# Attention beside a long convolution: the filters asked for among the first loads, and zero products on score banks

## The chip, the cores and the metric

The kernel runs on one core of a Trainium2 chip. The metric is device time of one execution in microseconds (us). "TensorE", "VectorE", "ScalarE", "GpSimd" and "SyncE" are the engines; the profile calls them PE (PEld for its weight loads), DVE, ACT, POOL and SP. A "q" behind the name, as in SPq, is the engine's queue issuing a transfer.

## The reference

Two independent halves, their outputs side by side. Length S = 2048, width D = 512, all in bf16.

```python
def _A_ref(x, wqkv, wo):                       # attention, H = 32 heads of 16
    q, k, v = (x @ wqkv), cut in three and into heads
    p = softmax(q k^T * 16 ** -0.5)
    return (p v) as (S, D) @ wo

def _B_ref(q, k, v, shift_k, ssm_k, ssm_D):    # gated long convolution, per channel
    k_shift[s] = sum over t < 4 of k[s - 3 + t] * shift_k[:, t'] 
    kv = k_shift * v
    y = causal convolution of kv with ssm_k (2048 taps per channel), + kv * ssm_D
    return q * y

out = concatenate([A, B], axis=-1)
```

## The kernel before

**Attention.** The scores are 2048 blocks of 128 keys by 512 queries, in 32 groups (4 query blocks by 8 groups of 4 heads). They are taken in *chunks* T of 3 blocks (2 in every second chunk up to `N_EARLY` = 56), 695 in all. For each chunk `emit_qk` issues the score products (L719) into PSUM banks 0 to 2 or 3 to 5 in turn, and ScalarE takes the exponential of the chunk into a tile PT (L726). From T = 16 on VectorE takes over one block of some chunks, by arithmetic of its own (L744 first, then the six passes of L784 to L791), in sets of two, later four; `dve_choice` decides by how far VectorE is behind in the plan. `emit_pv` (L835) multiplies the results with V into bank 6 (bank 7 for one group).

**Projections.** Jobs of Q, K and V products (`pe_unit` L401 and L408, `v_mm` L452) run in bank 5 early on, in bank 7 later, between score products; VectorE evicts them (L444, L462, L430). A job's next product waits until the bank is evicted.

**Convolution filters.** The filters `ssm_k` (512 channels by 2048 taps, 2 MB) come in two halves, `KZN[0]` (in tile QT) and `KZN[1]` (in tile EI), 1 MB each, with `DSS` (the 512 values of `ssm_D`, tile JNK). All three add to one semaphore, d_kz, and `h_kzl` is the third one's full count. GpSimd puts the first 128 taps into a small tile KZ0 and adds `DSS` (`kz_first`, L502 and L503). VectorE then turns the filters in 16 pieces of two halves each (`kz_turn`, L512 and L518) into a tile in WR, from where SyncE stores them to a scratch tensor in DRAM. The convolution (L992) reads shifted views of that scratch from T = 128 on.

**Order.** The program is written by a planner in plain Python. Every engine has a clock in it (`pe.t`, `act.t`, `dve.t`); each operation is appended to its engine's queue with a planned duration, and `when_of(h)` is the planned time of a result. On the chip each queue runs in order, waiting on semaphores. A transfer's planned landing is 4.0 us after its issue unless given. The pieces of the filters are appended at the end of a chunk's round:

```python
        while kv_pieces and T >= kv_pieces[0][0]:
            kv_pieces.pop(0)[1]()
        while kz_pieces and T >= kz_pieces[0][0] and (dve.t + kz_pieces[0][1] <= end + KZ_OVER or T >= kz_pieces[0][0] + 4):
            kz_pieces.pop(0)[2]()
```

`kv_pieces` holds `kz_first`, for T = 8. The `kz_pieces` are due at T = `KZ_AT` + 3i + j for piece i, half j, with `KZ_AT` = 11.

**First loads.** SyncE asks for: x rows 0 to 511, the transposes of x 512 to 1023, the second parts of WQ and WK (columns from 128), the transposes of x 1024 to 1535, `KZN[0]`, `KZN[1]`, `DSS`, the last transposes of x, then transposes of k and rows of v. ScalarE asks for: the first parts of WQ and WK, WV, the shift taps SHK; its table load and its first work stand behind these in its queue.

**Padding.** `keep_share` (L1160) adds products of zeros into a bank that is being accumulated, when the plan has TensorE busy under `SHARE` = 0.9 of the last `SPAN` = 3.4 us. `filler_home` names the bank, or None: between two groups, where the old group's last and the new group's first products with V are not both under way, there often is none, and nothing is added.

Of the kernel before, what the change touches and what calls it, by code (L numbers as in the profile page):

```python
# [6 lines left out]
ALU = mybir.AluOpType  # L7
# [35 lines left out]
N_EARLY = 56  # L43
# [38 lines left out]
SPAN = 3.4  # L82
SHARE = 0.9
# [14 lines left out]
SET_US = 0.72  # L98
PART_US = 0.6
KZ_US = .57  # L100
KZ_AT = 11
KZ_OVER = 0.0
FINISH = 8
TURN_BLKS = 9
TURN_AFTER = 4
STALL = 0.3
# [90 lines left out]
def bass_concat_heads__mha_block__ssm_conv_h3__prompt_kernel(  # L197
# [21 lines left out]
    def sem(name):  # L219
        return enter(nc.semaphore(name))  # L220
# [18 lines left out]
    ZR = sb("ZR", [128, 32])  # L239
# [4 lines left out]
    IDN = sb("IDN", [128, 128])  # L244
# [4 lines left out]
    KZ0 = sb("KZ0", [128, 4, 192])  # L249
# [31 lines left out]
    def dma(eng, dsem, outp, inp, deps=(), transpose=False, us=4.0, takes=0.0):  # L281
        h = dsem.add()

        def fn(e):
            f = e.dma_start_transpose if transpose else e.dma_start
            f(outp, inp).then_inc(dsem.sem, 16)  # L286
# [10 lines left out]
    def when_of(h):  # L297
        return at[(id(h[0]), h[1])] if h else 0.0
# [5 lines left out]
    d_tap, d_kz, d_wo = [DmaSem(sem(n)) for n in ("d_tap", "d_kz", "d_wo")]  # L304
# [18 lines left out]
    def load_x(sc):  # L323
        for c in range(4):
            h = turn_in(d_x[sc], xT[:, c, sc * 512:(sc + 1) * 512], x2[sc * 512:(sc + 1) * 512, 128 * c:128 * c + 128])
        h_x[sc] = [h]

    load_x(1)
    h_wv = dma(act, d_w[2], WV, wview[:, :, 2 * D:3 * D])
    h_shk = dma(act, d_tap, SHK[:, :, :], B_shift_k.rearrange("(c p) m -> p c m", p=128))  # L330
    h_wq.append(dma(sp, d_w[3], WQ[:, :, 128:D], wview[:, :, 128:D]))
    h_wk.append(dma(sp, d_w[4], WK[:, :, 128:D], wview[:, :, D + 128:2 * D]))
    load_x(2)
    kzview = B_ssm_k.rearrange("(p c) s -> p c s", c=4)
    for i in range(2):
        dma(sp, d_kz, KZN[i], kzview[:, 2 * i:2 * i + 2, :])
    h_kzl = dma(sp, d_kz, DSS, B_ssm_D.rearrange("(p c m) -> p c m", c=4, m=1))
    load_x(3)
    h_kt = {0: turn_in(d_kt[0], KTR[0][:, 16:LKT], k2[:, 0:128])}
    h_v2 = {0: dma(sp, d_v[0], VLO, v2[0:1024, :].rearrange("(t p) d -> p t d", p=128))}  # L340
# [154 lines left out]

    h_kzw = [None]

    h_kzt, h_kzs = [None], {}

    def kz_first():  # L500
        for i in range(2):
            h = pool.op(lambda e, i=i: e.tensor_copy(KZ0[:, 2 * i:2 * i + 2, 64:192], KZN[i][:, :, 0:128]), [h_kzl])  # L502
        h_kzt[0] = pool.op(lambda e: e.tensor_tensor(KZ0[:, :, 64:65], KZ0[:, :, 64:65], DSS, ALU.add), [h])  # L503

    def kz_turn(i, half):
        c, ro = i // VG, i % VG
        g0, g1 = (0, 24) if half == 0 else (24, NGR)
        o = 255 - ro - VG * g0
        k = KZN[c // 2][:, c % 2, o:o + 1]
        k = bass.AP(tensor=k.tensor, offset=k.offset, ap=[k.ap[0], [-VG, g1 - g0], [128, NB - 1], [-1, VG]])  # L510
        hs = [h_kzl, h_kzs.get(i - 4)]
        h = dve.op(lambda e: e.tensor_copy(KZS[:, i % 4, g0:g1, 1:NB, :], k), hs, us=KZ_US)  # L512
# [5 lines left out]
        h_kzp[i] = dve.op(lambda e: e.tensor_copy(KZS[:, i % 4, :, 0, :], k0), [h_kzt[0], h_kz0] + hs, us=0.19)  # L518
        kz_store(i)
        if i == 7:  # L520
            load_vhi()
# [17 lines left out]
    kz_pieces = [(KZ_AT + 3 * i + j, KZ_US + 0.22 * j, lambda i=i, j=j: kz_turn(i, j)) for i in range(16) for j in range(2)]  # L539
    kv_pieces.sort(key=lambda x: x[0])  # L540


# [19 lines left out]
    h = k_part(0, 128)  # L562
# [132 lines left out]
            chunk_of[b] = (T, j)  # L695
        chunks.append((bl, banks_of[T]))

    h_exp = {}
    h_blk = {}
    h_ptfree, pt_used = {}, {}  # L700

# [8 lines left out]
    def emit_qk(T):  # L710
        bl, banks = chunks[T]
        deps = qk_deps(T)
        assert None not in deps or T < 8

        def fn(e):
            ins = None
            for b, bank in zip(bl, banks):
                qb, g, kt, s = blk(b)
                ins = e.matmul(PS[:, bank, :],  # L719
                               lhsT=KTo[32 * s:32 * s + 32, g // 2, kt * 128:(kt + 1) * 128],  # L720
                               rhs=QT[32 * s:32 * s + 32, qb % 2, g, :],
                               start=True, stop=True, tile_position=(32 * s, 0))
            return ins
        h = pe.op(fn, deps, us=0.32)
        n = len(bl) - (bl[-1] in on_dve)
        h_exp[T] = act.op(lambda e: e.activation(PT[:, T % R_PT, 0:n * QB],  # L726
                                                 PS[:, banks[0]:banks[0] + n, :].rearrange("p b f -> p (b f)"),
                                                 ACT.Exp, scale=math.log(2.0) / OCT),
                          [h] + h_ptfree.get(T - R_PT, []), us=0.41 * n + 0.1)
# [415 lines left out]

    def keep_share(T, lim):
        home = filler_home(T)
        if home is None or T >= NT:
            return
        bank, col, start, dep = home  # L1150
        busy = sum(u for t, u in pe.last if t > lim - SPAN)
        n = blk_group(rest[0]) if rest else NQB * NG - 1
        turning = len(rest_of[n]) < 9 or len(rest_of[n]) > 4 * KT - 9
        us = min(lim - pe.t - 0.13, (1.0 if turning else SHARE) * SPAN - busy)
        while us > 0.08:
            k = min(max(int((us - 0.02) / 0.0565), 1), (512 - col) // 128)
# [6 lines left out]
            pe.op(fn, [h_zr, h_idn, dep], us=0.02 + 0.0565 * k)  # L1163

    def emit_bg(T, lim):
        bg_step(T, lim)
# [146 lines left out]
    for T in range(NT + 3):  # L1313
        if T < NT:
            take(T)
            for b in chunks[T][0]:
                pv_todo[blk_group(b)].append(b)
            emit_qk(T)
        lim = max(when_of(d) for d in qk_deps(T + 1)) if T + 1 < NT else pe.t + 1.0
        pvs = due_pvs(T, lim)  # L1320
        for b in [b for batch in pvs for b in batch]:
            n = blk_group(b)
            pv_todo[n].remove(b)
            pv_left[n] -= 1
            if not pv_left[n]:
                pv_done[n] = T
        early = False
        for batch in pvs:
            n = blk_group(batch[0])
            ready = max([when_of(h_blk[b]) for b in batch]  # L1330
                        + [when_of(bank_free[pvb(n)]) for b in batch if not in_bank.get((n, blk(b)[3]))])
            if T >= N_EARLY and not early and ready > pe.t + STALL:
                early = True
                emit_bg(T, ready)
            emit_pv(batch, T)
        if early:
# [90 lines left out]
```

## Time and profile before

| | |
|---|---|
| median of 3 runs | 832.82 us (829.57 to 833.69) |
| the profiled execution | 830.77 us |
| its span, first to last instruction | 828.9 us |
| ScalarE busy | 810.6 us (98%) |
| VectorE busy | 787.6 us (95%) |
| TensorE busy | 719.2 us (87%) |
| mean granted TensorE clock | 0.994 of full |

In the profile's rows a bracket such as [2.84 <-DMA JNK] is how long the engine stood idle ahead of the row, and what ended that. In rows of the timeline the first number is the start, the second the length that the merged instructions cover, both in us. In rows by line the numbers behind the bar are busy us, mean ns of one instruction, and idle us ahead of them. In rows by stretch (A:B) the busy times of PE, PEld, DVE, ACT and POOL stand in this order, then the granted clock, the share of the DMA engines, and GB/s.

### The profile page before, as it was taken

Reading aid. Unit: us, or ns where it says so; the run is one execution under the profiler, and the core shown is the slowest. Engines: PE = TensorE matmul, PEld = TensorE weight load, DVE = VectorE, ACT = ScalarE, POOL = GpSimd, SP = SyncE. Lnnn points to the kernel's source line nnn. Section 1 sums busy time; section 2 is a strip of 40 time slices with the busy share of each in tenths; the row PEclk is TensorE's granted clock in tenths of the full one; section 3 lists DMA queues with packets and bytes.
Section 4 is the critical chain, followed back from the end, with each engine's and each line's share of the span. In section 5 each row is a group of like instructions: output and inputs, shape, how many; then the busy total and the mean of one; then the engine's idle time right before and its main releaser. Section 6 shows DMA issues by size and latency. Waiting matters only on the chain.

```text
span 828.9 us, 29863 instructions
## 1 busy us (share of the span) xinstructions
PE 719.2 (87%) x13409; PEld 320.7 (39%) x13445; DVE 787.6 (95%) x1228; ACT 810.6 (98%) x702; POOL 17.3 (2%) x35
## 2 busy tenths in 40 slices
PE   8788899988888888888888888888888888988997
PEld 3233333334433443344344444344444443444222
DVE  3799999999999999999999999999999999999995
ACT  7899999999999999999999999999999999999997
POOL 3000000000000000000000000000000000000000
PEclk9999999999999999999999999999999998999999
DMA  9977602048736756499768788787789988775100
GB/s 244 288 253 269 178 1 48 30 98 282 235 95 195 219 184 216 138 259 296 233 210 274 234 260 263 231 254 238 226 264 307 274 286 299 229 225 187 26 1 26
DMA packets 123855, 167.30 MB, mean 202 GB/s; under 512 B 50384, under 2 KB 55504, under 8 KB 123472
## 3 DMA queue, kind: packets, MB, share of 16 engines
q1 hardware_dynamic: 120752, 162.77, 63.5%
q8 instruction: 106, 1.74, 0.8%
q10 hardware_dynamic: 2400, 1.05, 0.5%
q0 software_dynamic: 576, 1.57, 0.5%
q14 instruction: 21, 0.17, 0.1%
HBM read 143.14 MB, written 16.52 MB: 193 GB/s over the span
## 4 chain that ended last, share of the span: by engine, by line
ACT 88%; DVE 6%; PE 3%; SPq 2%; DMA 1%; issue 0%; POOL 0%; DVEq 0%
ACT PT L726 88%; DVE WR L512 2%; SPq L286 2%; DMA JNK<-in_B_ssm_D_dram 1%; PE PS L719 1%; PE PS L835 1%; DVE EI L744 1%; DVE KTo L444 0%; DVE KV L487 0%; DVE EA L787 0%; DVE WR L518 0%; DVE VAF L462 0%; PE PS L916 0%; DVE EA L784 0%; DVE EI L791 0%
## 5 line engine op out<-in xcount | busy, mean ns | idle before, releaser
L726 ACT ACTIVATE PT<-PS 128x1536 bf16<-128x1536 f32 (+1 forms) x695 | 806.5, 1432 | 7.3 <-PE PS L719 6.8
L719 PE MATMUL PS<-QT,KTo 32*128 32x512 bf16 x2048 | 273.0, 386 | 91.0 <-ACT PT L726 67.6
L835 PE MATMUL PS<-PT,VAF 128*32 128x512 bf16 x1782 | 227.8, 391 | 1.0 <-DVE STG L883 0.4
L992 PE MATMUL PS<-WR,KV 128*8 128x64 bf16 (+15 forms) x8192 | 182.7, 213 | 0.2
L992 PEld LDWEIGHTS PS<-WR,KV 128*18 128x18 bf16 (+15 forms) x8192 | 150.1, 119 | 43.9 <-issue 22.5
L719 PEld LDWEIGHTS PS<-QT,KTo 32*128 32x128 bf16 x2048 | 69.3, 91 | 243.2 <-ACT PT L726 224.0
L744 DVE TENSOR_SCALAR EI<-PS 128x512 int32<-128x512 f32 x206 | 136.6, 684 | 1.9 <-PE PS L719 1.2
L791 DVE SCALAR_TENSOR_TENSOR EI<-EI,EA 128x1024 int32<-128x1024 int32 (+1 forms) x90 | 92.1, 1040 | 0.0
L835 PEld LDWEIGHTS PS<-PT,VAF 128*32 128x32 bf16 x1782 | 53.4, 93 | 90.0 <-issue 84.0
L1160 PE MATMUL PS<-ZR,IDN 128*128 128x512 bf16 (+3 forms) x290 | 79.6, 329 | 0.2 <-issue 0.2
L790 DVE TENSOR_TENSOR EA<-EA,xT 128x1024 bf16<-128x1024 f16 (+1 forms) x53 | 46.7, 895 | 0.0
L835 PE MATMUL PS<-EI,VAF 128*32 128x512 bf16 x206 | 45.1, 411 | 1.8 <-DVE VAF L462 1.2
L787 DVE TENSOR_TENSOR EA<-EA,xT 128x1024 f16<-128x1024 f16 (+1 forms) x53 | 46.6, 896 | 0.0
L744 DVE TENSOR_SCALAR xT<-PS 128x512 int32<-128x512 f32 x60 | 39.9, 686 | 0.5 <-PE PS L719 0.2
L784 DVE TENSOR_SCALAR xT<-EI 128x1024 f16<-128x1024 uint16 (+1 forms) x46 | 37.8, 849 | 0.4
L1160 PEld LDWEIGHTS PS<-ZR,IDN 128*128 128x128 bf16 x290 | 22.7, 97 | 30.5 <-issue 20.4
L791 DVE SCALAR_TENSOR_TENSOR EI<-EI,WKV 128x1024 int32<-128x1024 int32 x28 | 34.1, 1219 | 0.0
L788 DVE TENSOR_SCALAR xT<-xT 128x1024 f16<-128x1024 f16 (+1 forms) x53 | 27.0, 527 | 0.0
L786 DVE TENSOR_SCALAR EA<-xT 128x1024 f16<-128x1024 f16 (+1 forms) x53 | 26.7, 527 | 0.0
L790 DVE TENSOR_TENSOR WKV<-WKV,STG 128x2048 bf16<-128x2048 f16 x21 | 25.5, 1215 | 0.0
L787 DVE TENSOR_TENSOR WKV<-WKV,STG 128x2048 f16<-128x2048 f16 x21 | 25.5, 1212 | 0.0
L883 DVE STREAM_TRANSPOSE STG<-PS 128x512 f32<-128x512 f32 x31 | 22.0, 711 | 2.8 <-PE PS L835 2.6
(87 smaller groups left out, 498.9 us busy)
## 6 DMA issues: line engine op xcount, KB each, us to landing
WR<-kz_scratch SPq DMA_DIRECT2D x512, 256.0 KB, 4.1
kz_scratch<-WR SPq DMA_DIRECT2D x16, 752.0 KB, 4.2
QN<-in_B_q_dram SPq DMA_DIRECT2D x16, 128.0 KB, 4.5
out_dram<-KV SPq DMA_DIRECT2D x16, 128.0 KB, 4.7
out_dram<-OUTA POOLq DMA_DIRECT2D x12, 128.0 KB, 3.7
QT<-in_B_ssm_k_dram SPq DMA_DIRECT2D x1, 1024.0 KB, 5.6
EI<-in_B_ssm_k_dram SPq DMA_DIRECT2D x1, 1024.0 KB, 8.8
STG<-in_B_v_dram SPq DMA_DIRECT2D x1, 1024.0 KB, 7.3
```

The lines of the kernel that those rows point to most:

```text
L719: ins = e.matmul(PS[:, bank, :], lhsT=KTo[32 * s:32 * s + 32, g // 2, kt * 128:(kt + 1) * 128], rhs=QT[32 * s:32 * s + 32, qb % 2, g, :], ...
L726: h_exp[T] = act.op(lambda e: e.activation(PT[:, T % R_PT, 0:n * QB], PS[:, banks[0]:banks[0] + n, :].rearrange("p b f -> p (b f)"), ACT.E ...
L744: s.fix.append(dve.op(lambda e: e.tensor_scalar(ei_of(i)[:, 0, :], PS[:, bank, :], FIX_LO, FIX_ADD, ALU.max, ALU.add), [h] + old + [x for ...
L784: step(2, lambda sl: lambda e: e.tensor_scalar(eb[:, sl], frac[:, sl], FS / OCT, -FS * ROOT0, ALU.mult, ALU.add), s.fix + old)
L786: step(4, lambda sl: lambda e: e.tensor_scalar(ea[:, sl], eb[:, sl], FS * (ROOT0 - ROOT1), None, ALU.add))
L787: step(2, lambda sl: lambda e: e.tensor_tensor(ea[:, sl], ea[:, sl], eb[:, sl], ALU.mult))
L788: step(4, lambda sl: lambda e: e.tensor_scalar(eb[:, sl], eb[:, sl], C1 * BITS / FS ** 3, (C0 + C1 * ROOT0) * BITS / FS ** 2, ALU.mult, AL ...
L790: step(2, lambda sl: lambda e: e.tensor_tensor(eg[:, sl], ea[:, sl], eb[:, sl], ALU.mult))
L791: step(1, lambda sl: lambda e: e.scalar_tensor_tensor(ei[:, sl], ei[:, sl], BITS / OCT, eg[:, sl], ALU.mult, ALU.add), ends=True)
L835: ins = e.matmul(PS[32 * s:32 * s + 32, pvb(qb * NG + g), :], lhsT=VAF[:, kt, h * VW:h * VW + 32], rhs=rhs, start=(order[b] == 0), stop=(o ...
L992: ins = e.matmul(PS[32 * c:32 * c + NW - 2 * n, BGB, col:col + 64], lhsT=KV[:, 2 * n:NW, 4 * qd + c], rhs=w, start=(n == 0), stop=(n == NB ...
L1160: return e.matmul(PS[:, bank, col:col + 128 * k], lhsT=IDN[:, :], rhs=ZR[:, :].rearrange("p (m d) -> p m d", m=1).broadcast_to([128, 4 * k ...
```

## The change

The two filter halves get a semaphore each. `DSS` and `KZN[0]` are asked for by ScalarE, behind SHK; `KZN[1]` by SyncE, behind the first transposes of x. The second x transposes come next, and the second parts of WQ and WK behind them. The planned landings of the halves are given, 11.5 and 14.5 on the plan's clock. `kz_first` is cut in two, one for each half, at T = 2 and T = 4. The pieces start at T = 4 in place of 11, in the same steps of three chunks, and each waits for its own half; a piece is appended only once the plan's VectorE clock has reached the half's planned landing less 0.1.

The second part: where `filler_home` gives None and T is 56 or more, zero products are added onto the first bank of the chunk's scores, behind the score products and ahead of the exponential, which then waits for them too. One is added as long as it ends in the plan 0.14 us before the exponential starts, and the busy share is under 0.9.

```diff
-KZ_AT = 11
+KZ_AT = 4
+KZ_LANDS = 11.5, 14.5
+ZERO_GAP = .14
...
     load_x(1)
     h_wv = dma(act, d_w[2], WV, wview[:, :, 2 * D:3 * D])
     h_shk = dma(act, d_tap, SHK[:, :, :], B_shift_k.rearrange("(c p) m -> p c m", p=128))
+    kzview = B_ssm_k.rearrange("(p c) s -> p c s", c=4)
+    dma(act, d_kz[0], DSS, B_ssm_D.rearrange("(p c m) -> p c m", c=4, m=1))
+    h_kzl = []
+    for i, q in enumerate((act, sp)):
+        h_kzl.append(dma(q, d_kz[i], KZN[i], kzview[:, 2 * i:2 * i + 2, :], us=KZ_LANDS[i] - q.t))
+    load_x(2)
     h_wq.append(dma(sp, d_w[3], WQ[:, :, 128:D], wview[:, :, 128:D]))
     h_wk.append(dma(sp, d_w[4], WK[:, :, 128:D], wview[:, :, D + 128:2 * D]))
-    load_x(2)
-    kzview = B_ssm_k.rearrange("(p c) s -> p c s", c=4)
-    for i in range(2):
-        dma(sp, d_kz, KZN[i], kzview[:, 2 * i:2 * i + 2, :])
-    h_kzl = dma(sp, d_kz, DSS, B_ssm_D.rearrange("(p c m) -> p c m", c=4, m=1))
     load_x(3)
...
-    def kz_first():
-        for i in range(2):
-            h = pool.op(lambda e, i=i: e.tensor_copy(KZ0[:, 2 * i:2 * i + 2, 64:192], KZN[i][:, :, 0:128]), [h_kzl])
-        h_kzt[0] = pool.op(lambda e: e.tensor_tensor(KZ0[:, :, 64:65], KZ0[:, :, 64:65], DSS, ALU.add), [h])
+    def kz_first(i):
+        cc = slice(2 * i, 2 * i + 2)
+        h = pool.op(lambda e: e.tensor_copy(KZ0[:, cc, 64:192], KZN[i][:, :, 0:128]), [h_kzl[i], h_kzl[0]])
+        h_kzt[i] = pool.op(lambda e: e.tensor_tensor(KZ0[:, cc, 64:65], KZ0[:, cc, 64:65], DSS[:, cc, :], ALU.add), [h])
...
-        hs = [h_kzl, h_kzs.get(i - 4)]
+        hs = [h_kzl[c // 2], h_kzs.get(i - 4)]
...
-    kv_pieces = [(8, kz_first)]
+    kv_pieces = [(KZ_AT - 2, lambda: kz_first(0)), (KZ_AT, lambda: kz_first(1))]
...
-                               start=True, stop=True, tile_position=(32 * s, 0))
+                               start=True, stop=bank != banks[0] or not fills.get(T), tile_position=(32 * s, 0))
...
+        exp_at[T] = act.t - (0.41 * n + 0.1)
...
     def keep_share(T, lim):
         home = filler_home(T)
-        if home is None or T >= NT:
+        if T >= NT:
+            return
+        if home is None:
+            zeros_on_scores(T, lim)
             return
...
+    def zeros_on_scores(T, lim):
+        if T < N_EARLY:
+            return
+        bank = chunks[T][1][0]
+        while True:
+            us = 0.02 + 0.0565 * 4
+            busy = sum(u for t, u in pe.last if t > lim - SPAN)
+            if pe.t + us > min(lim, exp_at[T] - ZERO_GAP) or busy > SHARE * SPAN:
+                return
+            fills.setdefault(T, []).append(len(fills.get(T, [])))
+            i = len(fills[T]) - 1
+
+            def fn(e, i=i):
+                return e.matmul(PS[:, bank, :], lhsT=IDN[:, :],
+                                rhs=ZR[:, :].rearrange("p (m d) -> p m d", m=1).broadcast_to([128, 16, 32]),
+                                start=False, stop=i == len(fills[T]) - 1)
+            h = pe.op(fn, [h_zr, h_idn], us=us)
+            act.ops[-1][0].append(h)
...
-        while kz_pieces and T >= kz_pieces[0][0] and (dve.t + kz_pieces[0][1] <= end + KZ_OVER or T >= kz_pieces[0][0] + 4):
+        while kz_pieces and T >= kz_pieces[0][0] and dve.t >= when_of(h_kzl[kz_pieces[0][3]]) - 0.1 and (dve.t + kz_pieces[0][1] <= end + KZ_OVER or T >= kz_pieces[0][0] + 4):
```

More of the change, by code (lines that the diff above doesn't have):

```diff
@@ L303, in bass_concat_heads__mha_block__ssm_conv_h3__prompt_kernel @@
     d_v = [DmaSem(sem(f"d_v{i}")) for i in range(2)]
-    d_tap, d_kz, d_wo = [DmaSem(sem(n)) for n in ("d_tap", "d_kz", "d_wo")]
+    d_tap, d_wo = [DmaSem(sem(n)) for n in ("d_tap", "d_wo")]
+    d_kz = [DmaSem(sem(f"d_kz{i}")) for i in range(2)]
     d_kzw = [DmaSem(sem(f"d_kzw{i}")) for i in range(4)]
@@ L496, in bass_concat_heads__mha_block__ssm_conv_h3__prompt_kernel @@
     h_kzw = [None]
-    h_kzt, h_kzs = [None], {}
-    def kz_first():
-        for i in range(2):
-            h = pool.op(lambda e, i=i: e.tensor_copy(KZ0[:, 2 * i:2 * i + 2, 64:192], KZN[i][:, :, 0:128]), [h_kzl])
-        h_kzt[0] = pool.op(lambda e: e.tensor_tensor(KZ0[:, :, 64:65], KZ0[:, :, 64:65], DSS, ALU.add), [h])
+    h_kzt, h_kzs = {}, {}
+    def kz_first(i):
+        cc = slice(2 * i, 2 * i + 2)
+        h = pool.op(lambda e: e.tensor_copy(KZ0[:, cc, 64:192], KZN[i][:, :, 0:128]), [h_kzl[i], h_kzl[0]])
+        h_kzt[i] = pool.op(lambda e: e.tensor_tensor(KZ0[:, cc, 64:65], KZ0[:, cc, 64:65], DSS[:, cc, :], ALU.add), [h])
     def kz_turn(i, half):
@@ L517, in kz_turn @@
         k0 = bass.AP(tensor=k0.tensor, offset=k0.offset, ap=[k0.ap[0], [-VG, NGR], [-1, VG]])
-        h_kzp[i] = dve.op(lambda e: e.tensor_copy(KZS[:, i % 4, :, 0, :], k0), [h_kzt[0], h_kz0] + hs, us=0.19)
+        h_kzp[i] = dve.op(lambda e: e.tensor_copy(KZS[:, i % 4, :, 0, :], k0), [h_kzt[c // 2], h_kz0] + hs, us=0.19)
         kz_store(i)
@@ L536, in load_vhi @@
         h_v2[1] = dma(sp, d_v[1], VHI, v2[1024:S, :].rearrange("(t p) d -> p t d", p=128), [h_kzp[7]])
-    kv_pieces = [(8, kz_first)]
-    kz_pieces = [(KZ_AT + 3 * i + j, KZ_US + 0.22 * j, lambda i=i, j=j: kz_turn(i, j)) for i in range(16) for j in range(2)]
+    kv_pieces = [(KZ_AT - 2, lambda: kz_first(0)), (KZ_AT, lambda: kz_first(1))]
+    kz_pieces = [(KZ_AT + 3 * i + j, KZ_US + 0.22 * j, lambda i=i, j=j: kz_turn(i, j), i // 8) for i in range(16) for j in range(2)]
     kv_pieces.sort(key=lambda x: x[0])
@@ L696, in take @@
         chunks.append((bl, banks_of[T]))
-    h_exp = {}
+    h_exp, exp_at, fills = {}, {}, {}
     h_blk = {}
@@ L1163, in keep_share @@
             pe.op(fn, [h_zr, h_idn, dep], us=0.02 + 0.0565 * k)
+    def zeros_on_scores(T, lim):
[15 more added lines that the diff above has]
+            act.ops[-1][0].append(h)
+            act.seen[id(h[0])] = h[1]
     def emit_bg(T, lim):
```

## The prediction

> **What bounds the kernel now.** I read the page first: span, busy line, the chain that ended last.
>
> ```profile
> span 828.9 us, 29863 instructions
> PE 719.2 (87%) x13409; PEld 320.7 (39%) x13445; DVE 787.6 (95%) x1228; ACT 810.6 (98%) x702; POOL 17.3 (2%) x35
> ACT 88%; DVE 6%; PE 3%; SPq 2%; DMA 1%; issue 0%; POOL 0%; DVEq 0%
> L726 ACT ACTIVATE PT<-PS 128x1536 bf16<-128x1536 f32 (+1 forms) x695 | 806.5, 1432 | 7.3 <-PE PS L719 6.8
> ```
>
> ScalarE is the bound: 695 exponentials fill 806.5 us, and its idle time ahead of them is 7.3 us in all. A change can win only that idle time, or hand blocks of scores from ScalarE to VectorE. So the second view is ScalarE's timeline, which starts a new row wherever the engine had stopped (the bracket is the stop).
>
> ```profile
> 5.99 1.09 ACT L387 ACTIVATE xT<-PS 128x512 bf16<-128x512 bf16 x2 [1.15 <-PE PS L382]
> ...
> 8.80 17.27 ACT L726 ACTIVATE PT<-PS 128x1536 bf16<-128x1536 f32 x15 [0.74 <-PE PS L719]
> 27.52 1.02 ACT L726 ACTIVATE PT<-PS 128x1024 bf16<-128x1024 f32 x1 [1.45 <-PE PS L719]
> 29.60 1.94 ACT L726 ACTIVATE PT<-PS 128x1024 bf16<-128x1024 f32 x2 [1.05 <-PE PS L719]
> 32.03 12.08 ACT L726 ACTIVATE PT<-PS 128x1024 bf16<-128x1024 f32 x11 [0.50 <-PE PS L719]
> 44.49 17.40 ACT L726 ACTIVATE PT<-PS 128x1024 bf16<-128x1024 f32 x16 [0.38 <-PE PS L719]
> ...
> 74.61 7.31 ACT L726 ACTIVATE PT<-PS 128x1536 bf16<-128x1536 f32 x6 [0.88 <-PE PS L719]
> 82.19 49.21 ACT L726 ACTIVATE PT<-PS 128x1536 bf16<-128x1536 f32 x41 [0.26 <-PE PS L719]
> ...
> 703.83 118.03 ACT L726 ACTIVATE PT<-PS 128x1024 bf16<-128x1024 f32 x102 [1.38 <-PE PS L719]
> ```
>
> Two places carry it. One lies between 26 and 32 us: 1.45 + 1.05 + 0.50 = 3.00 us, with smaller ones up to 82 us (0.38 + 0.88 + 0.26 = 1.52). The other is a single stop of 1.38 us at 703 us. The timeline of the other engines tells what the first is.
>
> ```profile
> 20.39 0.69 DVE L462 CAST VAF<-PS 128x512 bf16<-128x512 f32 x1 [1.85 <-PE PS L452]
> ...
> 23.91 1.18 DVE L512 COPY WR<-QT 128x1440 bf16<-128x1440 bf16 x2 [2.84 <-DMA JNK<-in_B_ssm_D_dram]
> ...
> 25.82 0.68 DVE L462 CAST VAF<-PS 128x512 bf16<-128x512 f32 x1
> ...
> 26.78 0.38 PE L408 MATMUL PS<-xT,WKV 128*128 128x512 bf16 x1 [2.51 <-DVE VAF L462]
> ```
>
> VectorE takes its queue in order. The first filter copy (L512) stands in it with a wait for all three filter loads, which share one semaphore; the last of them (JNK, the D row) lands at 23.9. Behind the copy stands the next V eviction (25.82). TensorE needs that eviction's bank for a K product and stands still for 2.51 us, and ScalarE runs dry. The stop is paid twice, because the granted clock then falls (the column after POOL):
>
> ```profile
> 24.00:26.00 2.00, 0.27 (x3) 0.00 (x0) 1.44 (x4) 2.00 (x2) 1.53 (x3) 1.00 1.03 204
> 28.00:30.00 2.00, 2.00 (x14) 0.33 (x12) 0.95 (x2) 0.95 (x2) 0.00 (x0) 0.50 0.97 306
> ```
>
> TensorE busy 0.27 of 2 us, and four us later half the clock.
>
> **The change, part by part.** *Loads earlier.* The queue of SyncE and the landings:
>
> ```profile
> 1.26 5.15 SPq L286 DMA_TRANSPOSE xT<-in_A_x_dram  x4
> ...
> 8.56 5.51 SPq L286 DMA_TRANSPOSE xT<-in_A_x_dram  x4
> 14.11 0.58 SPq L286 DMA_DIRECT2D QT<-in_B_ssm_k_dram  x1
> 14.73 0.43 SPq L286 DMA_DIRECT2D EI<-in_B_ssm_k_dram  x1
> ```
> ```profile
> QT<-in_B_ssm_k_dram SPq DMA_DIRECT2D x1, 1024.0 KB, 5.6
> EI<-in_B_ssm_k_dram SPq DMA_DIRECT2D x1, 1024.0 KB, 8.8
> ```
>
> Filter half 0 (QT) lands at 14.11 + 5.6 = 19.7 and half 1 (EI) at 14.73 + 8.8 = 23.5, so a megabyte takes 3.8 us behind another. After the change half 0 is asked for by ScalarE's queue behind WV and the taps, half 1 by SyncE's at 6.4, where the first transposes end. When does half 0 land? Its queue has to bring WV first:
>
> ```profile
> 2.67 0.64 ACTq L286 DMA_DIRECT2D SHK<-in_B_shift_k_dram  x1
> ...
> 9.76 0.33 PEld L452 LDWEIGHTS PS<-WKV,xT 128*128 128x128 bf16 x4 [0.23 <-DMA WKV<-in_A_wqkv_dram]
> ...
> 9.99 4.04 POOL L360 TENSOR_TENSOR OUTA<-IDN,SHK 128x512 bf16<-128x512 bf16 x4 [6.19 <-DMA SHK<-in_B_shift_k_dram]
> ...
> 14.73 0.69 DVE L462 CAST VAF<-PS 128x512 bf16<-128x512 f32 x1 [1.69 <-PE PS L452]
> ...
> 16.45 0.61 PE L408 MATMUL PS<-xT,WKV 128*128 128x512 bf16 x2
> ```
>
> WV is there at 9.76. With the engines to itself half 0 lands at 9.76 + 3.8 = 13.6; sharing them evenly with SyncE's queue, at 9.76 + 7.6 = 17.4. I take 15.5, the middle. The Trainium skill speaks against the second queue ("DMA: Bandwidth & Descriptors", Rules for kernel authors): loads issued from several engines run on the same 16 DMA engines and interleave, and only issue time is saved. By that rule half 0 comes at the late end, 17.4, and the sum is some 3 us higher; no run here has shown two such queues side by side yet, so it stands as the first rival.
>
> Exponentials take 17.27 / 15 = 1.15 us a chunk at the start, so chunk 4, where the copies may now begin, has its exponential at 8.80 + 4 x 1.15 = 13.4. A landing at 15.5 holds VectorE until then; the V eviction due at 14.73 slips behind the copy (about 0.65) to 16.2, and the product at 16.45 that needs its bank to about 16.9: TensorE loses 0.5 us. In the row above a loss of 2.51 cost ScalarE 1.45, so the first microsecond is absorbed. I take +0.4, with ends 0 (13.6) and +3.0 (17.4, the old stop in a new place). GpSimd's part (its KZ0 copies) stands behind its tap products, which end at 9.99 + 4.04 = 14.0; it adds under a microsecond and is inside this term.
>
> ScalarE issues two more loads, by the SyncE rows 0.6 and 0.5 us. Its first real work waited 1.15 us for TensorE (row 5.99), so this is covered; +0.1, ends 0 and +0.5. The loads moved back (the second part of WQ and WK, behind the second x transposes) are asked for some 6 us later; the first job that reads them is due four chunks ahead of block 128, about chunk 47, past 60 us: 0, ends 0 and +0.5. The second x transposes now stand behind half 1, which by the same two ends costs them 3.8 to 7.6 us; their last is issued at 14.07 now and the product of 26.78 is the first that reads them, 12.7 us later: 0.
>
> *The stop at 26 us.* With the filters there by 16 to 18, no copy waits, the eviction runs at about 24, and 3.00 us go. The smaller stops up to 82 us follow VectorE's lag of 2.84 us behind the order planned for it; half of 1.52 goes: -0.75, ends 0 and -1.5.
>
> *VectorE's idle time.*
>
> ```profile
> 11.00:23.90 12.90, 2.50 (x4) 1.00 1.09 266
> ```
> ```profile
> L512 DVE COPY WR<-QT 128x1440 bf16<-128x1440 bf16 x8 | 5.2, 649 | 2.8 <-DMA JNK<-in_B_ssm_D_dram 2.8
> L518 DVE COPY WR<-KZ 128x188 bf16<-128x188 bf16 x16 | 3.9, 243 | 0.6 <-POOL KZ L503 0.6
> L726 ACT ACTIVATE PT<-PS 128x1536 bf16<-128x1536 f32 x392 | 552.4, 1612 | 2.2 <-PE PS L719 1.9
> L726 ACT ACTIVATE PT<-PS 128x1024 bf16<-128x1024 f32 x303 | 308.4, 1198 | 5.1 <-PE PS L719 4.9
> ```
>
> VectorE worked 2.50 of the 12.9 us before the copies. The copies are still paced one pair in three chunks; only the start moves, by 7 chunks, which is 7 / 3 = 2.3 pairs of 2 x 0.65 + 0.24 = 1.55 us: 3.6 us of VectorE, not all 25. That is room for about one further block or pair in VectorE's share. A block less on ScalarE saves 552.4 / 392 - 308.4 / 303 = 0.39 us. I take -0.5; ends 0 (the planner finds no place) and -0.8 (one pair).
>
> *Zero products.* The stop at 703 us:
>
> ```profile
> 699.33 0.39 PE L719 MATMUL PS<-QT,KTo 32*128 32x512 bf16 x3 [0.34 <-ACT PT L726]
> 700.67 0.61 PE L719 MATMUL PS<-QT,KTo 32*128 32x512 bf16 x3 [0.95 <-ACT PT L726]
> ```
> ```profile
> 700.00:707.00 7.00, 6.33 (x101) 2.52 (x104) 6.16 (x9) 5.44 (x6) 0.00 (x0) 0.52 0.72 234
> ```
>
> Between two groups of heads TensorE has no product for a bank of its own to pad with, idles 0.34 and 0.95 us, and the clock stands at 0.52 until 707; ScalarE starves for 1.38 us. The change pads just there, on the score bank. -1.4, ends 0 (another turn dips) and -1.6. The Trainium skill ("TensorE: Matmul & The Clock Gate", the table of states) wants a whole idle window of about 3.4 us before the clock falls; by that no gap here is long enough, padding is worth nothing and the sum is 1.4 higher. The trace disagrees: the longest gap before the fall is 0.95 us. What the products cost: each is put in only where the plan has 0.246 + 0.14 us of room before its exponential, and where the stop between two chunks is mostly short that is seldom. 0, ends 0 and +0.9.
>
> The sum: 0.4 + 0.1 - 3.0 - 0.75 - 0.5 - 1.4 = -5.15. The profiled execution took 830.77 (span 828.9 and 1.87 around it), 2.05 below the median of the runs shown, 832.82. Forecast 830.77 - 5.15 = 825.6. About 0.5%, 4.2 us, is what a measurement of this kernel tells from no change; against the median the forecast is 0.87% lower.
>
> **The rivals.** *The stop only moves* (chance 0.22). Half 0 lands at 17 or later, copy, V eviction and K product queue up behind it as they do now at 24, and the clock falls again: +3.0 in place of +0.4, so 828.2; with the dip at a turn not mended either, 829.6. For it: two streams on the same engines, and a clock that falls after such a stop. Against it: the eviction at 14.73 is not needed before 16.45.
>
> *Only the load matters* (0.15). The first stop goes, but the planner finds no block for VectorE, the later stops stay and a turn still dips: 830.77 - 3.0 + 0.5 = 828.3. For it: the stops at 74 and 82 us lie 45 us behind the first and may have causes of their own. Against it: a queue that starts 2.84 us late stays late while it is full.
>
> *Zero products hold the exponentials: slower* (0.10). ScalarE has no slack against TensorE after 82 us, and each product puts a further wait before an exponential. There are about 30 turns of two to three chunks, some 75 exponentials. At 0.07 us each the gain of 5.15 is gone; at 0.15 the time is 825.6 + 11 = 837. For it: a TensorE that runs a little behind the plan would show at once. Against it: the room asked for.
>
> **How the numbers follow.** The forecast's case holds 0.53 and gives 822 to 828 by its terms (all good ends: 3.0 + 1.5 + 0.8 + 1.6 = 6.9, so 823.9; a run or two lower, as runs of this kernel lie within 829.57 to 833.69). The two rivals without change of sign end at 828 to 830, so the range is 821.5 to 831.5, which leaves the slow rival out. Faster by over 0.5% (below 828.7): 0.53 and some of the two milder rivals, 0.61; within: 0.28; slower: 0.11.
>
> **What would show it.** Right: no stop of ScalarE above 0.5 us between 9 and 32 us; the first L512 row near 13 to 16 us, with a wait under 2.5 us; clock 1.00 throughout 24 to 34 us; a few products into PS from ZR at the score turns and no exponential that waits for them; one or two blocks more in L744. Wrong: L512 waiting for the QT load over 2.5 us and L408 for VAF right behind it; ScalarE rows after 82 us that begin with a wait for the zero products; a new row with clock 0.5.

## The result: 1% slower, and the profile after

The changed kernel takes 840.07 us (median of 6 runs, 835.65 to 844.55) against 831.5 (829.57 to 833.69): ratio 1.0101, 95% interval 1.0077 to 1.0126. A second comparison on another chip gave 1.0121 (1.0103 to 1.0138). The profiled execution is the fastest of the six, 835.65 with a span of 833.8. Times below are medians, and the bracket behind a ratio is its 95% interval. Two executions further down stand far above their fellows (2279.26 us with the landings planned late, 855.12 us at a mean clock of 0.656 with the loads back and the k transposes later) and are left out of the medians, while one of 851.23 us at a clock of 0.746, in the changed kernel without zero products, is counted.

Line numbers move by a few. In the changed kernel the score products are L723, the exponentials L730, VectorE's first step on a block L749, the filter copies L516 and L522, K products L412, V evictions L466, zero products on score banks L1186. The page of the changed kernel:

```profile
span 833.8 us, 29887 instructions
PE 720.2 (86%) x13414; PEld 318.2 (38%) x13449; DVE 789.1 (95%) x1227; ACT 811.1 (97%) x702; POOL 16.9 (2%) x36
...
ACT 88%; DVE 5%; SPq 4%; PE 2%; issue 0%; DMA 0%; DVEq 0%
...
L730 ACT ACTIVATE PT<-PS 128x1536 bf16<-128x1536 f32 (+1 forms) x695 | 807.1, 1392 | 11.3 <-PE PS L723 10.6
```

The exponentials take the same time to 0.6 us; ScalarE's idle time ahead of them grew from 7.3 to 11.3 us, and SyncE's queue has 4% of the chain that ended last in place of 2%. ScalarE's timeline tells where:

```profile
9.03 22.08 ACT L730 ACTIVATE PT<-PS 128x1536 bf16<-128x1536 f32 x20 [0.75 <-PE PS L723]
37.74 1.45 ACT L730 ACTIVATE PT<-PS 128x1536 bf16<-128x1536 f32 x1 [6.63 <-PE PS L723]
40.65 14.51 ACT L730 ACTIVATE PT<-PS 128x1024 bf16<-128x1024 f32 x13 [1.46 <-PE PS L723]
...
75.76 3.78 ACT L730 ACTIVATE PT<-PS 128x1024 bf16<-128x1024 f32 x4 [0.50 <-PE PS L723]
80.01 479.55 ACT L730 ACTIVATE PT<-PS 128x1536 bf16<-128x1536 f32 x408 [0.46 <-PE PS L723]
560.07 266.68 ACT L730 ACTIVATE PT<-PS 128x1024 bf16<-128x1024 f32 x231 [0.52 <-PE PS L723]
```

The stops at 26 to 32 us are gone: twenty exponentials run on from 9.03 to 31.1. So is the stop at 703. But between 31 and 41 there is a new one of 6.63 + 1.46 = 8.09 us. The timeline of the other engines, around it:

```profile
13.24 1.43 DVE L516 COPY WR<-QT 128x1440 bf16<-128x1440 bf16 x1
...
26.05 5.32 SPq L288 DMA_TRANSPOSE WR<-in_B_k_dram  x1
...
31.41 13.77 SPq L288 DMA_DIRECT2D kz_scratch<-WR  x7
35.21 0.98 DVE L516 COPY WR<-QT 128x1440 bf16<-128x1440 bf16 x2 [6.91 <-DMA kz_scratch<-WR]
...
37.09 0.61 PE L723 MATMUL PS<-QT,KTo 32*128 32x512 bf16 x3 [6.84 <-DVE EI L749]
```

Read it from below. TensorE waits 6.84 us for VectorE's step on a block of scores, which frees the bank. That step stands in VectorE's queue behind a filter copy, and the copy waits 6.91 us for a *store* of the filters, not for a load. The copies go through four slots (`KZS[:, i % 4]`); the fifth piece writes over the first, and must wait until store 0 has landed. The copy of piece 0 was done at 16.2, but store 0 is issued by SyncE, behind two transposes of k and a load of v: issued at 31.41, landed at 35.2. Before, store 0 was no earlier, as SyncE's timeline of the kernel before shows:

```profile
26.18 6.51 SPq L286 DMA_TRANSPOSE WR<-in_B_k_dram  x1
32.73 11.31 SPq L286 DMA_DIRECT2D kz_scratch<-WR  x6
```

But there the fifth piece came seven chunks later, at 39.02, after that store had landed (36.45). In the changed kernel the clock then falls, as it did in the old stop (the granted clock stands behind the five busy times):

```profile
32.00:34.00 2.00, 0.00 (x0) 0.00 (x0) 0.00 (x0) 0.00 (x0) 0.00 (x0) 1.00 1.18 395
36.00:38.00 2.00, 0.91 (x6) 0.24 (x6) 2.00 (x5) 0.26 (x1) 0.00 (x0) 0.50 0.99 412
```

The ledger below is summed from ScalarE's rows in each trace (us): the start of the first exponential, the sum of the exponentials, ScalarE's idle time among them ahead of 100 us and behind it, and the rest of the span.

| profile | first at | busy | idle to 100 | idle past 100 | rest | span |
|---|---|---|---|---|---|---|
| before | 8.80 | 806.5 | 4.96 | 1.58 | 7.1 | 828.9 |
| changed | 9.03 | 807.1 | 9.86 | 0.72 | 7.1 | 833.8 |
| changed, second chip (839.6 us, its median) | 9.59 | 807.4 | 11.12 | 2.63 | 7.1 | 837.8 |

So the lost 4.9 us of the first pair lie in the early idle time: -3.00 for the old stop, +8.09 for the new one, -0.19 for all smaller ones together. The usual execution loses some 4 us more, with a lower mean clock (0.982 to 0.992 in five runs, 0.994 in the profiled one). The second chip's profile, at the usual time, has them at these places: 0.56 us at the start, 1.26 in the early idle time, 1.91 in the late one.

### The profile page after: what moved, and what is told of

Same layout as the page of the kernel before. It is cut to its first block, busy times and chain, and to the rows that moved or that the text cites. A ratio compares the mean times of both kernels' runs of the same rounds, so it can differ in the third digit from the quotient of the medians.

```text
span 833.8 us, 29887 instructions
## 1 busy us (share of the span) xinstructions
PE 720.2 (86%) x13414; PEld 318.2 (38%) x13449; DVE 789.1 (95%) x1227; ACT 811.1 (97%) x702; POOL 16.9 (2%) x36
## 4 chain that ended last, share of the span: by engine, by line
ACT 88%; DVE 5%; SPq 4%; PE 2%; issue 0%; DMA 0%; DVEq 0%
ACT PT L730 88%; SPq L288 4%; DVE WR L516 1%; PE PS L723 1%; PE PS L840 0%; DVE EI L796 0%; DMA kz_scratch<-WR 0%; DVE EI L749 0%; DVE KTo L448 0%; PE PS L405 0%; DVE VAF L466 0%; DVE KV L491 0%; PE PS L456 0%; DVE xT L749 0%; PE PS L479 0%
## 5 line engine op out<-in xcount | busy, mean ns | idle before, releaser
L730 ACT ACTIVATE PT<-PS 128x1536 bf16<-128x1536 f32 (+1 forms) x695 | 807.1, 1392 | 11.3 <-PE PS L723 10.6
L723 PE MATMUL PS<-QT,KTo 32*128 32x512 bf16 x2048 | 272.8, 385 | 95.6 <-ACT PT L730 63.6
L997 PE MATMUL PS<-WR,KV 128*26 128x64 bf16 (+15 forms) x8192 | 179.6, 214 | 1.5 <-issue 0.9
L723 PEld LDWEIGHTS PS<-QT,KTo 32*128 32x128 bf16 x2048 | 69.9, 91 | 251.2 <-ACT PT L730 221.2
L997 PEld LDWEIGHTS PS<-WR,KV 128*28 128x28 bf16 (+15 forms) x8192 | 146.4, 119 | 46.6 <-issue 24.6
L749 DVE TENSOR_SCALAR EI<-PS 128x512 int32<-128x512 f32 x206 | 136.9, 684 | 2.6 <-PE PS L723 2.3
L749 DVE TENSOR_SCALAR xT<-PS 128x512 int32<-128x512 f32 x60 | 39.5, 682 | 0.6 <-PE PS L723 0.4
```

Of the source, the lines that this page charges most:

```text
L723: ins = e.matmul(PS[:, bank, :], lhsT=KTo[32 * s:32 * s + 32, g // 2, kt * 128:(kt + 1) * 128], rhs=QT[32 * s:32 * s + 32, qb % 2, g, :], ...
L749: s.fix.append(dve.op(lambda e: e.tensor_scalar(ei_of(i)[:, 0, :], PS[:, bank, :], FIX_LO, FIX_ADD, ALU.max, ALU.add), [h] + old + [x for ...
L997: ins = e.matmul(PS[32 * c:32 * c + NW - 2 * n, BGB, col:col + 64], lhsT=KV[:, 2 * n:NW, 4 * qd + c], rhs=w, start=(n == 0), stop=(n == NB ...
```

## The experiments

Theory A: store 0 stands in SyncE's queue behind the k transposes. Rivals: B, the early loads crowd out others; C, the zero products hold the exponentials. The kernel before, run beside these, took 829.2 to 830.3.

**The k transposes behind the fourth store.**

```diff
-    h_kt = {0: turn_in(...)}; h_v2 = {0: dma(sp, ...)}; h_kt[1] = turn_in(...)
+    def load_k(): the same three            # called in kz_store at i == 3
```

> The changed kernel, with the two transposes of k and the load of v moved in SyncE's queue from ahead of all filter stores to behind the fourth store. Theory A (store 0 stands in SyncE's queue behind the k transposes until 31.4 us, lands at 35.2, and the fifth copy piece, which reuses its slot, holds VectorE for 6.9 us): the stop of 6.63 + 1.46 us on ScalarE goes, no L516 row waits for a store over 1 us, and the time falls from 840 by 8 us or more, to 826 to 832. Theory B (the early filter loads crowd out other loads): the stop or one like it stays, 836 to 844. Theory C (the zero products hold the exponentials): 838 to 842.

834.37 us, ratio 1.0069 (1.0047 to 1.0091). No copy waits for a store, the stop of 8 us is gone: A's mechanism holds. But the time is above the range given: some 5 us of the 840 came back, not the 8 or more. Its ledger: first at 9.01, idle to 100 6.16, past 100 2.23. In this execution half 0 landed late, the first copy waited 2.36 us for it, and the clock stood at half from 18.3 us for 10.2 us.

**The copies at chunk 11, the loads early.**

```diff
-KZ_AT = 4
+KZ_AT = 11
```

> The changed kernel with the copies starting at chunk 11 as before, in place of 4; the loads stay early. Theory A: the fifth piece comes 7 chunks later, at about 9.0 + 23 x 1.15 = 35.5 us, when store 0 has just landed (35.2), so the wait is under 1 us, the first stop of before is gone as well, and the time is 827 to 831. Theory B: the loads are as early, so 836 to 844. Theory C: 838 to 842.

827.52 us (12 runs), ratio 0.9994 (0.9976 to 1.0013). The loads are as early here as in the changed kernel and nothing is lost, so B falls as the main cause. The profiled execution was its slowest, 833.81: there half 0 landed late (15.7), the fifth and sixth piece did wait for stores, 1.0 and 1.2 us, and the clock stood at half from 41.9 us for 17.1 us.

**The zero products alone, on the kernel before.**

```diff
+            zeros_on_scores(T, lim)      # with exp_at, fills and the stop flag
```

> The kernel before with the zero products on score banks alone; loads and copies as before. Theory A: few products are added (3 in the changed kernel), so within 0.3% of before, at most 1.4 us faster by a turn without a clock dip. Theory C: slower than before by 0.5% to 1%, 836 to 840.

829.73 us, ratio 1.0006 (0.9986 to 1.0026). C falls here: two products, at 701 us, are all that the plan has room for.

**The changed kernel without them.**

```diff
-            zeros_on_scores(T, lim)
```

> The changed kernel without the zero products on score banks. Theory A: as the changed kernel, 836 to 844, with the same stop at 31 to 38 us. Theory C: 829 to 834.

842.48 us, ratio 1.0178 (1.0144 to 1.0213); the stop of 7.13 + 1.45 us is there. C falls once more: without them the time is no lower, so they are no part of the loss.

**The first four stores on GpSimd's queue.**

```diff
-        h_kzs[i] = dma(sp, d_kzw[i % 4], ...
+        h_kzs[i] = dma(pool if i < 4 else sp, (d_kzp if i < 4 else d_kzw)[i % 4], ...
```

> The changed kernel with the first four filter stores issued by GpSimd's queue in place of SyncE's, everything else where it was. Theory A (store 0 waits in SyncE's queue behind the k transposes): store 0 goes out when its copy ends, about 16.3 us, no copy waits for a store over 1 us, the stop of 6.6 us on ScalarE goes, and the time falls by about as much as with the k transposes moved: 831 to 836. Rival (the store itself is slow, whatever queue): the fifth piece still waits over 3 us, 837 or more.

834.51 us, ratio 1.0072 (1.0042 to 1.0102). As A said, by a second route: store 0's place in the queue was the cause, not the store itself. Store 0 goes out at 17.0, the fifth piece waits for nothing, no copy waits for a store over 1.6 us (1 was expected), and the stop moved on. The timeline:

```profile
23.70 12.26 SPq L288 DMA_TRANSPOSE WR<-in_B_k_dram  x1
...
36.19 0.62 DVE L517 COPY WR<-QT 128x1440 bf16<-128x1440 bf16 x1 [1.57 <-DMA kz_scratch<-WR]
...
38.17 1.36 PE L413 MATMUL PS<-xT,WKV 128*128 128x512 bf16 x3 [4.51 <-DMA xT<-in_A_x_dram]
40.12 1.02 ACT L731 ACTIVATE PT<-PS 128x1024 bf16<-128x1024 f32 x1 [4.97 <-PE PS L724]
```

With the stores now on GpSimd's queue, one transpose of k keeps SyncE's queue for 12.26 us (2.42 in the changed kernel), and the last transposes of x, issued by 23.7, land at 38.0 (25.4 there), 4.5 us too late for a K product: ScalarE stands for 4.97 us. That the stores slow the transposes is argued from their falling together; no run takes them apart.

**Planned landings as late as the real ones.** On the first of these kernels:

```diff
-KZ_LANDS = 11.5, 14.5
+KZ_LANDS = 16.5, 18.5
```

> The kernel with the k transposes behind the fourth store, and with the planned landings of the filter halves moved from 11.5 and 14.5 to 16.5 and 18.5, as they landed in two of the profiles (15.6 and 18.5). Copies then start about four chunks later. Theory D (what is left of the loss with the stores freed, 834.4 against 827.5 for copies at chunk 11, is the wait for half 0 in executions where it lands late, and the clock that falls after it): the stops before 32 us go and the time is 827 to 829. Theory E (the loss comes from later: the plan that follows from early copies has wider gaps on TensorE at group turns and more clock dips): 832 to 836.

834.89 us (five runs), ratio 1.0067 (1.0045 to 1.0089). Half 0 landed at 17.0 here. Theory D falls as the whole cause: the copies waited for no load, and the time is the same. The k transposes, now behind store 3, hold the *next* stores: copy 8 waits for store 4 (SyncE's and VectorE's timelines).

```profile
37.70 5.95 SPq L288 DMA_TRANSPOSE WR<-in_B_k_dram  x1
43.69 3.46 SPq L288 DMA_DIRECT2D kz_scratch<-WR  x4
```
```profile
47.45 0.54 DVE L519 COPY WR<-EI 128x1440 bf16<-128x1440 bf16 x1 [2.44 <-DMA kz_scratch<-WR]
```

Behind it TensorE stands for 3.12 us, and ScalarE for 3.31 at 51.9 us.

**Both: k transposes later, copies at chunk 11.**

```diff
-KZ_AT = 4
+KZ_AT = 11
...      # and load_k() behind the fourth store
```

> The k transposes behind the fourth store and the copies from chunk 11: no copy waits for a load or a store. Theory A with D or E: 825 to 828, the fastest so far, by up to 1 us under the 827.5 of copies at chunk 11 alone, with fewer slow executions among its runs (there the fifth and sixth piece waited 1.0 and 1.2 us for stores).

828.58 us, ratio 0.9989 (0.9967 to 1.001), above the range given and not faster than the copies at chunk 11 alone. What the early loads can cost is seen here (waits of 9 to 60 us): at 17.9 a K product had waited 2.0 us for the first transposes of x, and ScalarE stood 1.24 us at 18.6 and 1.08 at 23.3.

```profile
PE PS L415 <- DMA xT<-in_A_x_dram: 2.0, 1, 2.0
```

**The changed kernel again.**

> The changed kernel once more, beside the others on the same chip: 836 to 844, with the stop at 31 to 38 us and, in its profile, landings of half 0 either near 13.2 or near 15.7 us.

839.58 us, ratio 1.0121 (1.0103 to 1.0138), the stop 7.51 + 1.45 us. The wait of the fifth piece was 7.8 us.

**The filter loads back in their place.** Of the change stay the semaphore for each half, the planned landings and the zero products.

```diff
-KZ_AT = 4
-KZ_LANDS = 11.5, 14.5
+KZ_AT = 11
+KZ_LANDS = 19.5, 23.3
...      # DSS, KZN[0], KZN[1] on SyncE behind load_x(2); WQ, WK ahead of it, as before
```

> The changed kernel with the filter loads back where they were before (SyncE's queue, behind WQ, WK and the second x transposes), the D row ahead of half 0, a semaphore for each half, planned landings 19.5 and 23.3, copies from chunk 11. Theory F (the first stop came from one semaphore for three loads: the first copy needs half 0 alone, which lands at 19.7, ahead of its place at 21 to 24): the stop at 26 to 32 us goes without any load moved, 826 to 829. Rival (only loads asked for earlier cure it): the stop stays, 829 to 831.

826.83 us (826.4 to 827.08), ratio 0.9968 (0.9956 to 0.9979): the lowest median here, faster than both, with the narrowest spread (of five runs; the intervals of the four other kernels with the loads in this place overlap its own). ScalarE's timeline has no stop above 0.88 us to the end of the exponentials:

```profile
8.76 32.34 ACT L730 ACTIVATE PT<-PS 128x1536 bf16<-128x1536 f32 x29 [0.75 <-PE PS L723]
41.72 17.41 ACT L730 ACTIVATE PT<-PS 128x1024 bf16<-128x1024 f32 x16 [0.63 <-PE PS L723]
...
71.85 7.31 ACT L730 ACTIVATE PT<-PS 128x1536 bf16<-128x1536 f32 x6 [0.88 <-PE PS L723]
79.42 738.07 ACT L730 ACTIVATE PT<-PS 128x1536 bf16<-128x1536 f32 x633 [0.26 <-PE PS L723]
```

and the first copy needs no earlier load (GpSimd's and VectorE's timelines): half 0 is there at 20.27, the copy comes at 20.95, and half 1, at 23.7, holds no copy.

```profile
20.27 0.40 POOL L506 COPY KZ<-QT 128x256 bf16<-128x256 bf16 x1 [6.01 <-DMA QT<-in_B_ssm_k_dram]
...
23.70 0.40 POOL L506 COPY KZ<-EI 128x256 bf16<-128x256 bf16 x1 [2.75 <-DMA EI<-in_B_ssm_k_dram]
```
```profile
20.95 0.97 DVE L516 COPY WR<-QT 128x1440 bf16<-128x1440 bf16 x2
```

**The same with the k transposes later.**

```diff
+        if i == 3:
+            load_k()
```

> As the one before it, and the k transposes behind the fourth store. Theory A: no copy waits for a store either; 825 to 828, and no product waits for x, as it did for 2.0 us (K product at 18 us) with the filter loads early. If moving the k transposes matters little once the copies start at chunk 11: within 0.1% of the one before it.

827.41 us (six runs), ratio 0.9974 (0.9963 to 0.9985): no gain over the one before it. With copies from chunk 11 the stores are early enough where they are.

**The kernel before with only the k transposes later.**

```diff
+        if i == 3:
+            load_k()
```

> The kernel before with only the k transposes behind the fourth store. Theory A: the fifth copy came at 37 us there and its store had landed, so nothing is gained: the stop of 3.0 us at 26 to 32 us stays, 828 to 831.

830.56 us, ratio 1.0011 (0.9999 to 1.0023); the old stop is there (1.61 + 1.17 us at 28 to 30). As expected.

**Four early copies, the rest as before.**

```diff
-kz_pieces = [(KZ_AT + 3 * i + j, ...
+kz_pieces = [((KZ_AT if i < 4 else 11) + 3 * i + j, ...
```

> The changed kernel with only the first four pieces (as many as there are slots) from chunk 4; the other twelve start at chunk 23 and on, as before. Theory A: the early copies fill the slots, none waits for a store over 1.2 us, the stop of 6.6 us goes: 826 to 831. Theory E (early copies as such lead to a plan with more clock dips after 100 us): 831 to 834, with clock dips after 100 us and no stop before.

831.52 us, ratio 1.0029 (1.0009 to 1.0049). The slots are filled early and nothing waits long (1.21 us at most): 8.1 us less than the changed kernel run again (839.58, on another chip; by the ratios 1.0029 for 1.0121), from one number. Idle to 100 is 2.81 us, 2.15 less than before. Idle past 100 is 4.26, against 1.58: that part of theory E is seen. The largest stop there is not at a turn between two groups; TensorE and then the clock:

```profile
520.49 0.37 PE L997 MATMUL PS<-WR,KV 128*24 128x64 bf16 x13 [1.94 <-issue]
```
```profile
518.00:520.00 2.00, 0.54 (x18) 0.35 (x16) 2.00 (x3) 2.00 (x2) 0.00 (x0) 1.00 0.14 44
522.00:524.00 2.00, 2.00 (x18) 0.52 (x13) 1.87 (x3) 1.07 (x2) 0.00 (x0) 0.50 0.48 131
```

In the middle of a convolution step TensorE waited 1.94 us for nothing that the view names. More on that at the end.

**Loads in place, no zero products.**

```diff
-            zeros_on_scores(T, lim)
```

> Filter loads in their old place, a semaphore for each half, planned landings 19.5 and 23.3, copies from chunk 11, without the zero products. Theory Z (two zero products at about 697 us keep the clock from falling at that turn): a dip near 700 us comes back in some executions, 827 to 829, with a wider spread than the 826.4 to 827.1 with them. Rival (they do nothing here): 826.4 to 827.1 as with them.

828.18 us (826.6 to 831.35), ratio 0.9976 (0.9957 to 0.9994). The stop at the turn near 700 us is back, 1.38 us at 703.9, and the spread is wider, as Z said.

**Loads in place, the semaphores alone.**

```diff
-        h_kzl.append(dma(sp, d_kz[i], KZN[i], ..., us=KZ_LANDS[i] - sp.t))
+        h_kzl.append(dma(sp, d_kz[i], KZN[i], ..., us=4.0))
...      # no gate on the planned landing, no zero products
```

> As the one before it, with the planned landing of 4.0 us after the issue as in the kernel before and no gate on it: only the semaphores and the two halves of kz_first are left. Theory F (the semaphore for three loads made the stop): as the one before it, within 0.1%, no stop at 26 to 32 us. Rival (the plan's knowledge of the landing does it): the stop of 3.0 us is back, 829 to 831.

828.13 us, ratio 0.9971 (0.9952 to 0.9989): the same as with the landings planned (828.18), and no stop at 26 to 32 us. Theory F holds: the old stop came from one semaphore for three loads. (The D row is asked for ahead of the halves here too, but that alone would not do it: under one semaphore the copy would have waited for half 1, which landed at 23.55 in the kernel before, 0.34 us ahead of the D row. `kz_first` stays cut in two, one part for each semaphore.)

**Four early copies, padded to a share of 1.0, and the control.**

```diff
-SHARE = 0.9
+SHARE = 1.0
```

> The kernel with only the first four pieces from chunk 4, and the busy share up to which zeros are padded raised from 0.9 to 1.0. Theory E (the loss left over is the clock dips after 100 us): fewer dips, mean clock 0.998 or more, 827 to 830. Rival (the loss is elsewhere): 831 or more, at whatever clock.

> The control: the kernel with the filter loads in their old place and padding up to a share of 1.0. There the clock hardly falls, so padding has nothing to win: 826 to 828; if more zeros delay score products it is slower than that.

831.99 us (ratio 1.0035, 1.0003 to 1.0067) and 828.01 (0.9971, 0.995 to 0.9991). The first lies above the 827 to 830 of theory E, the control at the end of its 826 to 828. Padding does not lift the clock of the early plan (mean over its runs 0.993, as without), so it tells nothing of what the dips cost; but the one run of the early plan at clock 1.0 has a span of 827.0 us, 1.9 above the 825.1 of the control's run at clock 1.0. From one run each, the dips are not all of it.

## Why the prediction was wrong, step by step

Forecast 825.6, faster (0.61); measured 840.07, slower, outside the range of 821.5 to 831.5.

- **The step that failed**: "With the filters there by 16 to 18, no copy waits". In the profile of the changed kernel no copy waited for a filter (on the second chip one did, 1.0 us), but the fifth piece waited 6.91 us for a store. I followed the copies upstream, to the loads, and not downstream, to the slots that they fill: four slots, emptied by stores that SyncE issues behind its k transposes. A step moved forward by 7 chunks passes everything that it shares a queue or a buffer with. The term of -3.00 was right for its own stop, and should have stood beside +8.09. The rows for it were in the trace of before: store 0 issued at 32.73 behind a transpose that held SyncE for 6.51 us. This term makes up most of the 8 us between the changed kernel and the one with four early copies: the early idle time is 9.86 and 11.12 in the two profiles of the one, 2.81 in the other. The signs that I had named for this part (no stop up to 32 us, first copy at 13 to 16, clock 1.00 up to 34 us) all came true; they ended just ahead of the new stop.
- **The landing** (15.5, ends 13.6 and 17.4). Over the ten profiles with early loads half 0 lands anywhere from 12.6 to 17.4. Half 0 was asked for at 4.33; in the profile of the changed kernel (first fence) it landed at 13.2, in that of the first experiment (second fence), asked for at 4.32, at 15.6:

```profile
QT<-in_B_ssm_k_dram ACTq DMA_DIRECT2D x1, 1024.0 KB, 8.9
```
```profile
QT<-in_B_ssm_k_dram ACTq DMA_DIRECT2D x1, 1024.0 KB, 11.3
```

  So 15.5 was a fair middle, and each single landing is luck; what sets it, the runs do not tell. The rule of the Trainium skill on two queues ("DMA: Bandwidth & Descriptors", Rules for kernel authors) says that loads from several engines run on the same DMA engines and interleave. I had read the late end, 17.4, out of it, and the 12.6 to 17.4 do not bear that out as the usual case. That the loads share the engines agrees with another row: the first transposes of x, issued from 1.3 us on in every profile, land at 10.5 to 10.8 in the eight profiles with the loads in their old place, and at 12.9 to 17.8 in these ten. The prediction has no term for them, and one was missing: in three of the ten, where they landed at 16.0 or later, a product waited for them, 2.0 us at the most. My "0" for the second transposes held, no product waited for those.
- **The smaller stops** (-0.75): not shown. All stops up to 100 us but the large ones sum to 1.96 us before and 1.77 in the changed kernel, and to 2.37 with the loads back and the old stop gone; there the stop of 0.88 us at 72 stays. So they do not follow from VectorE's lag behind the first copy.
- **VectorE's room** (-0.5): 0. It takes 206 + 60 = 266 blocks before and after (the x counts of L744 before and of L749 after), though the copies moved 7 chunks.

```profile
L744 DVE TENSOR_SCALAR EI<-PS 128x512 int32<-128x512 f32 x206 | 136.6, 684 | 1.9 <-PE PS L719 1.2
L744 DVE TENSOR_SCALAR xT<-PS 128x512 int32<-128x512 f32 x60 | 39.9, 686 | 0.5 <-PE PS L719 0.2
```
```profile
L749 DVE TENSOR_SCALAR EI<-PS 128x512 int32<-128x512 f32 x206 | 136.9, 684 | 2.6 <-PE PS L723 2.3
L749 DVE TENSOR_SCALAR xT<-PS 128x512 int32<-128x512 f32 x60 | 39.5, 682 | 0.6 <-PE PS L723 0.4
```

- **ScalarE's two issues** (+0.1): the first exponential starts at 9.03 for 8.80. But over all profiles it starts at 8.99 to 9.59 with early loads and at 8.76 to 9.53 without, so +0.23 is inside the scatter and the term is not told from 0.
- **The zero products** (-1.4): the mechanism was right. Near 700 us, in the plan with copies from chunk 11, the clock falls in all four profiles without them (before, and three experiments) and in none of the six with them; against their cost my 0 holds, three are issued in the changed kernel. In the time it is not shown: alone they changed nothing (1.0006), and with the loads back the intervals with and without them overlap.
- **The rivals.** "The stop only moves" came nearest: it does move, but to a place I had not looked at, and it grew. The slow rival, zero products that hold exponentials, was the wrong one.
- **What stays open.** The changed kernel's usual run is some 4 us above its profiled one, and the plans with early copies stand idle for 0.7 to 4.4 us past 100 us (2.6 in the mean of eight profiles), against 0.1 to 3.2 (1.0 in the mean of ten) with copies from chunk 11. Their clock is lower: with the same early loads, 0.990 in the mean of the first experiment's runs, 0.998 with copies at chunk 11. Moving the stores out of the way left the time 0.7% above the kernel before, by both routes. Why that plan meets more dips of the clock, the runs do not settle; padding up to a full share did not cure it.

## What to carry to other kernels

When a producer is moved earlier, follow its output too: which buffer it fills, who empties that, and what stands ahead of the emptying in *its* queue. Before moving loads, look at what the waiting instruction really waits for: here one semaphore shared by three loads made a copy wait 2.84 us for data that it did not read. Splitting it gave 0.3%; moving the 2 MB of loads forward gave nothing that could be measured (0.9994 with the copies in their old place), and starting the copies earlier as well cost 1%. A planner that believes in a queue without delays (SyncE's stores here) will place work by it; check each buffer's last reader against the trace, not the plan.

## What the hardware showed that I had not expected

The clock falls and rises in steps: but for the fall at the very end of the program, the time at half clock (0.5) comes in pieces of 3.4, 6.8, 10.2 or 17.1 us, and within a profile the falls start whole multiples of 3.413 us apart. It can fall without any long gap. In the second profile of the changed kernel no gap of TensorE between 654 and 660 us was over 0.51 us, but it was busy for 1.06 us of two, and that was enough:

```profile
656.00:658.00 2.00, 1.06 (x40) 0.51 (x31) 2.00 (x3) 2.00 (x3) 0.00 (x0) 1.00 0.84 242
660.00:662.00 2.00, 2.00 (x18) 0.33 (x10) 0.79 (x2) 1.19 (x2) 0.00 (x0) 0.50 0.95 267
```

Counted from the clock records of the 18 profiles, there are 29 such falls, in 16 of them, and in the 3.413 us ahead of each TensorE was busy for 0 to 67%. Of the 3732 stretches on the same grid without a fall behind them, 14 were as low as that. So in this kernel the busy share of one stretch goes with the fall, not the longest gap, and it matters where the grid happens to cut a thin place. The grid lies differently from one execution to the next: the first rise of the clock comes anywhere from 4.0 to 6.9 us.

The Trainium skill ("TensorE: Matmul & The Clock Gate", Part 1) has a window of some 3.4 us, with which the pieces agree, and its table of states asks for at least one idle window before the clock falls, with which these rows do not.

A transpose on its way in holds its queue longer when other traffic runs. Four transposes of x (512 rows each) kept SyncE's queue for 5.15 us at the start of the kernel before, and the next four for 5.51 us; behind half 1 these took 8.34 us in the changed kernel and 12.19 with the landings planned late. The first transpose of k (2048 rows) took 2.42 us in the changed kernel, and 12.26 beside the four stores on GpSimd's queue.

The stop of 1.94 us at 518.5 us, with four early copies, has a neighbour in the DMA records: a transfer of 16 KB on the queue that the page calls "instruction" runs from 518.15 to 519.09. Between 100 and 815 us the 18 profiles hold 12 stops of TensorE over 1 us. Three are the same wait for ScalarE at 790 to 797 us; the nine others all begin within 0.6 us of the end of such a transfer, of which there is one in some 7 us. That speaks for instructions that arrive late; no run here tests it.
